# Top-k attention and mixture of depths: the mask moved from the scores into PSUM

## The chip, the cores and the metric

The kernel runs on one core of one Trainium2 chip. The metric is the time of one execution on the device in microseconds (us). Each of the core's engines runs its own queue of instructions in order: TensorE (PE in the profile; its weight loads are PEld), VectorE (DVE), ScalarE (ACT), GpSimd (POOL), and SyncE (SP), which here only issues transfers. They wait for each other through semaphores. TensorE writes PSUM; VectorE and ScalarE read PSUM and SBUF; GpSimd works in SBUF.

## What is computed

Eight batches, eight heads, 576 tokens, head width 64. In each row of the attention scores only the 32 largest entries survive, the rest is set to a very low value, and a softmax and the product with v follow. The heads are put side by side to rows of 512, and a "mixture of depths" layer picks 128 tokens in each batch by a gate score and adds a two-layer perceptron to them.

```python
scores = scale * np.matmul(q, k.transpose(0, 1, 3, 2))
kth = np.partition(scores, -top_k, axis=-1)[..., -top_k:-top_k + 1]
scores = np.where(scores >= kth, scores, -1000000000.0)
attn = np.exp(scores - max); attn /= sum(attn)
x = matmul(attn, v), heads side by side                # (8, 576, 512)
top_idx = 128 tokens with the largest x @ w_gate       # in each batch
out = x;  out[top_idx] += sigmoid(gate) * (relu(x[top_idx] @ w1) @ w2)
```

Everything is float32.

## The kernel before, in words

**Tiles.** The 576 query tokens of a batch are cut into four tiles of 128 (`t` = 0 to 3) and one of 64 (`t` = 4). A *unit* is one tile for one pair of heads: 8 batches x 5 tiles x 4 pairs = 160 units, 20 to a batch. A unit of a 128-token tile holds two score tiles of 128 x 576, one for each head; a unit of the 64-token tile packs both heads into the partitions of one score tile. So there are 288 score tiles in all.

**Steps.** The main loop (line 664) runs over steps `n`. In each step several units are worked on, each at another stage. A unit `u` passes through:

- step u-1: `multiply` (line 258): TensorE makes the scores in PSUM (`ps`); `keep` (line 275): ScalarE copies them to SBUF (`sc`);
- step u: `find_bound` (line 285): VectorE finds a bound below which few candidates lie, by many MAX8 and MATCH_REPLACE8 instructions on strips; `cut` (line 306): ScalarE rounds it into `seen`;
- step u+1: `part` (line 313): ScalarE takes the Sign of each score against the bound (`sides`) and the count; GpSimd multiplies scores by it (`y`) and appends 8 filler columns (`fill`, line 328); `find_kth` (line 337): one MAX8 of VectorE on each tile gives eight values, the last of them the 32nd largest score; `lift` (line 344): GpSimd multiplies it by 2^90 (BIG) into `seen`;
- step u+2 (lines 724 to 737): ScalarE makes Relu(2^90 (kth - score)), GpSimd subtracts it from the scores: `z`, the masked scores;
- step u+3: `turn` (line 347) and `turn_last` (line 355): TensorE transposes z into PSUM (`ptr`; the last columns into a corner of `ps`); ScalarE applies exp on the way out (`pT`, `last`);
- step u+4: `values` (line 365): TensorE multiplies by v (`av`); `keep_values` (line 401): ScalarE copies that to `xs`.

The scores are scaled down by 2^-20 when q is loaded, and exp's scale undoes it; they are not shifted by their row maximum. With v stands a column of ones, which gives the softmax's sum.

**Order.** `pe`, `dve`, `act`, `pool` and `sp` are wrappers (class `InOrder`, line 34) that pin each instruction behind the one traced before it on its engine, so every engine's queue runs in the order of the code. For ScalarE a step is: Signs of n-1, exps of n-3, copies that were put off (`flush`), Relus of n-2, score copies of n+1, value copy of n-4, cut of n. For TensorE: for each of two score tiles, transposes of n-3 and values of n-4; then scores of n+1; then a piece of the mixture or of the next batch's load. For GpSimd: y of n-1, fill, z of n-2, normalising, lift. For VectorE: bound of n, 32nd largest of n-1, then the small work of gates, normalising and routing. PSUM holds one buffer each for scores, values and the small pieces and two for transposes.

**Beside the units.** The loads of the next batch's k and q (`load_kq`, line 170) are cut into nine pieces with TensorE transposes, one each in the steps of `load_at`; v follows at step `v_at` of the batch. When a batch's last tile is normalised and its gates are known, it is stored to DRAM, and `mixture` (line 492) is run in pieces, one a step: route, pick, gather with an indirect transfer, two matmul layers in four and three pieces, and an indirect add into the output.

**The end.** After the loop a chain of checks (`sure`) looks at the smallest and largest of the recorded bounds, counts and sums; where they could not be trusted, a general routine (line 852) computes everything again. It is not entered with these inputs.

Of the kernel before, what the change touches and what calls it, by code (L numbers as in the profile page):

```python
# [9 lines left out]
AF = mybir.ActivationFunctionType  # L10
ALU = mybir.AluOpType
# [7 lines left out]
CAP = 128  # L19
# [26 lines left out]
def kernel(  # L46
# [56 lines left out]

    NS = B * NHP * (2 * J + 1)
    seen = const.tile([P, 3, NS], FP32, name="seen")
# [205 lines left out]
    def part(i, sc, at, sides):  # L313

        act.activation(
            sides[:, i, :],  # L320
            sc[:, i, :],
            AF.Sign,
            bias=seen[:, 0, at + i : at + i + 1],
            scale=-(1.0 + 2.0**-23),
            accum_out=seen[:, 2, at + i : at + i + 1],
        )

    def fill(n, y, at):

        pool.tensor_tensor(  # L330
            y[:, 0:n, S : S + 8],
            steps[:, 0:n, :],
            seen[:, 2, at : at + n].unsqueeze(2).to_broadcast([P, n, 8]),
            ALU.subtract,
        )

    def find_kth(n, y):

        next8 = stats.tile([P, 2, 8], FP32, name="next8")
        for i in range(n):  # L340
            dve.max(next8[:, i, :], y[:, i, :])
        return next8

    def lift(n, next8, at):
        pool.tensor_scalar_mul(seen[:, 1, at : at + n], next8[:, 0:n, 7], BIG)

    def turn(i, z):

        tr = ps_tr.tile([P, 512], FP32, name="ptr")
        for c in range(J):  # L350
            at = c * P + i * R
            pe.transpose(tr[:, c * P : (c + 1) * P], z[:, i, at : at + P], ident)
        return tr

    def turn_last(n, z, ps):

        last = z.rearrange("p i s -> p (i s)")[:, JP : JP + n * R]  # L360
        tr = ps[0 : n * R, 1, 1, 512 - P : 512]
        pe.transpose(tr, last, ident)
        return tr
# [91 lines left out]
    def break_ties(t, gate, gate_row, rank):  # L455

        n = R if t == J else P
        work = wkpool.tile([P, 2, S], FP32, name="ties", tag="z")
        tok_row = modpool.tile([P, S], I32, name="tok_row", tag="scratch")
        nc.gpsimd.iota(  # L460
            tok_row[:, 0:JP].rearrange("p (j i) -> p j i", j=J),
            pattern=[[1, J], [J, P]],
            base=0,
            channel_multiplier=0,
        )
        nc.gpsimd.iota(
            tok_row[:, JP:S], pattern=[[1, R]], base=JP, channel_multiplier=0
        )
        nc.vector.tensor_copy(out=work[:, 0, :], in_=tok_row)
        tok = stats.tile([P, 2], FP32, name="tok")  # L470
        nc.vector.tensor_copy(out=tok[0:n, 0:1], in_=tok_i[0:n, t : t + 1])
        nc.vector.tensor_scalar(
            out=work[0:n, 1, :],
            in0=gate_row[0:n, :],
            scalar1=gate[0:n, t : t + 1],
            scalar2=None,
            op0=ALU.is_equal,
        )
        nc.vector.scalar_tensor_tensor(
            out=work[0:n, 0, :],  # L480
            in0=work[0:n, 0, :],
            scalar=tok[0:n, 0:1],
            in1=work[0:n, 1, :],
            op0=ALU.is_lt,
            op1=ALU.mult,
            accum_out=tok[0:n, 1:2],
        )
        nc.vector.tensor_tensor(
            rank[0:n, t : t + 1], rank[0:n, t : t + 1], tok[0:n, 1:2], ALU.add
        )  # L490

    def mixture(row0, x, gate, rank, exact=False):
# [9 lines left out]
        pick = modpool.tile([P, NT, CAP], FP32, name="pick")  # L502
# [140 lines left out]
    load_at = (1, 2, 3, 4, 7, 8, 9, 11, 12)  # L643
    first_load_at = (5, 6, 7, 8, 9, 10, 11, 12, 13)
    v_at = 6
    mix_from = 5
# [12 lines left out]
    scs, bests, zs, weights = {}, {}, {}, {}  # L659
# [4 lines left out]
    for n in range(-1, len(units) + 6):  # L664
# [10 lines left out]
        if tiles_of(n - 3):  # L675
            pT = ptpool.tile([P, 2, J, P], FP32, name="pT")
            last = ptpool.tile([P, P], FP32, name="last")
            z, trs = zs.pop(n - 3), []
        if tiles_of(n - 4):
            b4, t4, hp4 = units[n - 4]  # L680
            av = ps_av.tile([P, 512], FP32, name="av")
        if tiles_of(n - 3) or tiles_of(n + 1):
            ps = room_for_scores()
        for i in range(2):
            if i < tiles_of(n - 3):
                trs.append(turn(i, z))
                if i == tiles_of(n - 3) - 1:
                    trs.append(turn_last(i + 1, z, ps))
            if i < tiles_of(n - 4):
                values(t4, hp4, i, *weights[n - 4], av, qkv[b4][2])  # L690
# [6 lines left out]
        if tiles_of(n - 1):  # L697
# [8 lines left out]
            next8 = find_kth(tiles_of(n - 1), y)  # L706
        if tiles_of(n - 3):
            w = tiles_of(n - 3)
# [8 lines left out]
            weights[n - 3] = pT, last  # L717
# [4 lines left out]


        if tiles_of(n - 2):
            sc = scs.pop(n - 2)
            z = wkpool.tile([P, 2, S], FP32, name="z")
            at = first_tile[n - 2]
            for i in range(tiles_of(n - 2)):
                act.activation(
                    z[:, i, :],  # L730
                    sc[:, i, :],
                    AF.Relu,
                    bias=seen[:, 1, at + i : at + i + 1],
                    scale=-BIG,
                )
                pool.tensor_tensor(z[:, i, :], sc[:, i, :], z[:, i, :], ALU.subtract)
            zs[n - 2] = z
        if tiles_of(n + 1):
            scs[n + 1] = keep(tiles_of(n + 1), ps)
        if tiles_of(n - 4):  # L740
            b, t, hp = b4, t4, hp4
# [5 lines left out]
            weights.pop(n - 4)  # L747
# [10 lines left out]
        b, i = divmod(n, per_batch)  # L758
        if i >= mix_from or b > 0:
            next(mixing, None)  # L760
# [6 lines left out]
        if tiles_of(n - 4):  # L767
            b, t, hp = units[n - 4]
            if hp == NHP - 1:
                normalising = b, t, xs, x, gate  # L770
        if tiles_of(n - 1):
            lift(tiles_of(n - 1), next8, first_tile[n - 1])
        b, i = divmod(n, per_batch)
        if n >= 0 and b + 1 < B:
            steps_of_load = first_load_at if b == 0 else load_at
            if i == steps_of_load[0] - 1:
                qkv[b + 1] = room_for_qkv(b + 1)
                loading = load_kq(k[b + 1], q[b + 1], *qkv[b + 1][0:2])
                next(loading)
            if i in steps_of_load:  # L780
                next(loading)
            if i == v_at:
                load_v(v[b + 1], qkv[b + 1][2])
# [8 lines left out]
    for what, op, than, limit in (  # L792
        (seen[:, 0, :], ALU.min, ALU.is_gt, LEAST),
        (seen[:, 1, :], ALU.min, ALU.is_gt, LEAST * BIG),
        (seen[:, 2, :], ALU.max, ALU.is_lt, float(MIDDLE)),
        (seen[:, 2, :], ALU.min, ALU.is_gt, float(MIDDLE - 16)),
# [27 lines left out]
    def general_weights(n, sc):  # L824

        p = wkpool.tile([P, 2, S], FP32, name="p", tag="z")
        for i in range(n):
            cur, tops = sc[:, i, :], []
            left = wkpool.tile([P, 2, S], FP32, name="left", tag="z")
# [100 lines left out]
```

## Time and profile before

| | us |
|---|---|
| median of 3 runs | 1160.65 (1156.92 to 1163.18) |
| the profiled execution's own time | 1161.06 |
| its span (first to last instruction) | 1158.6 |
| TensorE / VectorE busy | 985.9 (85%) / 910.0 (79%) |
| ScalarE / GpSimd busy | 879.7 (76%) / 905.8 (78%) |
| granted TensorE clock, mean | 0.878 of full |
| transfers | 42 GB/s mean |

Groups of instructions that the change touches (busy time in all, mean length of one):

| engine, instruction | count | busy us | mean ns |
|---|---|---|---|
| GpSimd, subtraction z | 288 | 407.7 | 1434 |
| GpSimd, lift (two columns / one) | 128 / 32 | 37.4 / 7.4 | 292 / 231 |
| GpSimd, product y | 288 | 363.0 | 1279 |
| ScalarE, Relu z | 288 | 210.5 | 783 |
| ScalarE, Sign | 288 | 221.1 | 768 |
| TensorE, transposes of z (`ptr`) | 1152 | 206.5 | 308 |
| TensorE, transposes of the last columns (`ps`) | 160 | 48.4 | 305 and 292 |

The reader should know four things. Nearly every line of the profile says L42, since all of it goes through the wrapper; the tiles' names tell the groups apart. A group's busy time is a union: where instructions of other groups overlap, both are counted, and on the pipelined TensorE the mean length of one is longer than the spacing of two. "idle before, releaser" tells for what an engine waited. The clock row tells how much of TensorE's full clock was granted; at 0.5 its matmuls take twice as long.

### The profile page before, as it was taken

What the parts mean: (1) busy time and instruction counts of PE and PEld (TensorE: products, weight loads), DVE (VectorE), ACT (ScalarE), POOL (GpSimd) and SP (SyncE); (2) the same over time, 40 slices, a digit from 0 to 9 for tenths busy, and PEclk for the clock granted to TensorE, in tenths of its full rate; (3) what the DMA queues carried; (4) which work ended last, traced back from release to release, by engine and by line L of the source; (5) the groups of instructions that cost most, each with busy time, mean ns of one, the idle gap of its engine ahead of it and who ended that gap; (6) DMA issues with size and microseconds to landing.
All of it is one profiled execution on the core that took longest, in us unless ns stands there. A gap on an engine that the chain in (4) does not pass through costs nothing.

```text
span 1158.6 us, 23113 instructions
## 1 busy us (share of the span) xinstructions
PE 985.9 (85%) x6906; PEld 820.3 (71%) x6906; DVE 910.0 (79%) x4980; ACT 879.7 (76%) x2113; POOL 905.8 (78%) x974
## 2 busy tenths in 40 slices
PE   6788878899789988899888998889987898778946
PEld 3566657787677876778677786678766787667845
DVE  5888788787897778976898868978789777898640
ACT  4898798696978769777786878969797876978721
POOL 3999798797978769777787878879797887878820
PEclk9898897799977989779886899969998788978978
DMA  5641022100411013110141101410041001000020
GB/s 121 199 100 28 1 80 63 36 2 11 114 38 29 1 17 108 38 28 1 21 114 28 28 1 34 119 28 11 9 110 26 10 1 47 5 1 10 1 60 13
DMA packets 123829, 49.03 MB, mean 42 GB/s; under 512 B 118960, under 2 KB 118960, under 8 KB 122672
## 3 DMA queue, kind: packets, MB, share of 16 engines
q1 hardware_dynamic: 120320, 42.88, 14.4%
q0 software_dynamic: 1792, 4.20, 2.1%
q8 instruction: 58, 0.95, 0.3%
q14 instruction: 75, 0.61, 0.2%
q10 hardware_dynamic: 1584, 0.39, 0.2%
HBM read 35.91 MB, written 11.53 MB: 41 GB/s over the span
## 4 chain that ended last, share of the span: by engine, by line
PE 51%; ACT 20%; POOL 19%; DVE 5%; issue 4%; DMA 1%; POOLq 0%; ACTq 0%
PE av L42 18%; PE ps L42 13%; POOL y L42 9%; PE ptr L42 9%; POOL z L42 8%; PE h_ps L42 6%; ACT sides L42 6%; ACT sc L42 5%; PE y_ps L42 4%; ACT pT L42 3%; ACT z L42 3%; PE extra_ps L42 2%; DVE prod L42 1%; DVE next L42 1%; POOL out_dram L607 1%
## 5 line engine op out<-in xcount | busy, mean ns | idle before, releaser
L42 POOL TENSOR_TENSOR z<-sc,z 128x576 f32<-128x576 f32 x288 | 407.7, 1434 | 62.9 <-ACT z L42 61.9
L42 POOL TENSOR_TENSOR y<-sc,sides 128x576 f32<-128x576 f32 x288 | 363.0, 1279 | 116.9 <-ACT sides L42 109.1
L42 DVE MAX8 cand<-sc 128x8 f32<-128x72 f32 x2304 | 323.5, 216 | 89.9 <-ACT sc L42 89.4
L42 PE MATMUL av<-v,pT 128*128 128x65 f32 (+1 forms) x2560 | 340.9, 283 | 5.5 <-ACT xs L42 5.2
L42 PEld LDWEIGHTS av<-v,pT 128*128 128x128 f32 (+1 forms) x2560 | 324.2, 203 | 18.4 <-ACT xs L42 10.2
L42 PE MATMUL ptr<-ident,z 128*128 128x128 f32 x1152 | 206.5, 308 | 113.7 <-POOL z L42 113.7
L42 DVE MAX8 next<-y 128x8 f32<-128x584 f32 x288 | 207.8, 759 | 98.9 <-POOL y L42 97.6
L42 PE MATMUL ps<-kT,qT 64*128 64x288 f32 (+1 forms) x1280 | 232.4, 488 | 21.3 <-ACT last L42 16.6
L42 ACT COPY sc<-ps 128x576 f32<-128x576 f32 x288 | 171.7, 647 | 99.6 <-PE ps L42 99.5
L42 PEld LDWEIGHTS ptr<-ident,z 128*128 128x128 f32 x1152 | 146.0, 159 | 142.4 <-POOL z L42 139.1
L42 ACT ACTIVATE pT<-ptr 128x512 f32<-128x512 f32 x288 | 163.0, 585 | 88.4 <-PE ptr L42 87.8
L42 ACT ACTIVATE sides<-sc,seen 128x576 bf16<-128x576 f32 x288 | 221.1, 768 | 4.9
L42 ACT ACTIVATE z<-sc,seen 128x576 f32<-128x576 f32 x288 | 210.5, 783 | 1.4 <-POOL seen L42 1.4
L42 PEld LDWEIGHTS ps<-kT,qT 64*128 64x128 f32 (+1 forms) x1280 | 119.5, 203 | 73.2 <-ACT last L42 30.2
L42 DVE MAX8 best<-cand 128x8 f32<-128x64 f32 x864 | 154.2, 215 | 3.3
L42 DVE MATCH_REPLACE8 cand<-best,cand 128x64 f32<-128x64 f32 x576 | 116.5, 209 | 0.0
L42 PEld LDWEIGHTS h_ps<-xeT,w 128*128 128x128 f32 x512 | 64.7, 205 | 16.6 <-issue 11.8
L42 DVE CUSTOM_DVE_ANT_0 prod<-x,wg 128x512 f32<-128x512 f32 (+1 forms) x40 | 72.1, 1802 | 4.5 <-POOL x L42 4.5
L42 PE MATMUL h_ps<-xeT,w 128*128 128x128 f32 x512 | 70.9, 296 | 2.1 <-ACT hT L42 1.4
L42 PE MATMUL y_ps<-w,hT 128*128 128x192 f32 (+1 forms) x384 | 62.2, 315 | 1.5 <-ACT gy L42 1.1
L42 PE MATMUL av<-vpair,last 128*128 128x130 f32 x256 | 63.4, 333 | 0.0
L42 PEld LDWEIGHTS y_ps<-w,hT 128*128 128x128 f32 x384 | 56.1, 190 | 10.1 <-issue 7.7
(74 smaller groups left out, 859.3 us busy)
## 6 DMA issues: line engine op xcount, KB each, us to landing
rows<-in_k_dram SPq DMA_DIRECT2D x64, 128.0 KB, 2.8
v<-in_v_dram SPq DMA_DIRECT2D x64, 128.0 KB, 3.0
out_dram<-x SPq DMA_DIRECT2D x8, 1024.0 KB, 4.7
rows<-in_q_dram SPq DMA_DIRECT2D x62, 128.0 KB, 2.9
w<-in_moe_w_dram SPq DMA_DIRECT2D x2, 2048.0 KB, 14.0
last<-in_k_dram SPq DMA_DIRECT2D x8, 128.0 KB, 3.1
vlast<-in_v_dram SPq DMA_DIRECT2D x8, 128.0 KB, 3.7
vpair<-in_v_dram SPq DMA_DIRECT2D x16, 64.0 KB, 3.1
```

The source lines that it names most:

```text
L42: return lambda *a, **kw: self._tc.keep_in_program_order(fn(*a, **kw))
L607: nc.gpsimd.indirect_dma_start(out=out.flatten_outer_dims(), out_offset=bass.IndirectOffsetOnAxis(ap=row_i, axis=0), in_=gy, in_offset=Non ...
```

## The change

The scores are no longer masked in SBUF. A new `mask` makes a small bf16 tile `less` in the step of the turn: for a unit's first score tile ScalarE takes Relu(kth - score), which is positive where the score lies below the 32nd largest and zero elsewhere; for the second score tile GpSimd compares (`is_lt`, 1 or 0). TensorE transposes the unmasked scores, and behind each transpose one bf16 matmul of `less` with a constant `out_of_reach` (the identity times -2^90) adds the transposed mask to the same place in PSUM; exp then gives zero for what is masked. The 32nd largest values are read straight from `next8`, now one constant tile for all units; `lift` is gone, and `seen` holds two rows.

A unit's stages become five: scores, bound, part, mask and turn, values. The stage of z falls away, so the turn is done at u+2 and the values at u+3. The order on ScalarE in a step is: the mask's Relu of n-2, Signs of n-1, exps of n-2, copies that were put off, score copies of n+1, value copy of n-3, cut of n. On GpSimd: comparison of n-2, y of n-1, fill, normalising. On TensorE each transpose is followed by its mask matmul. Loads and mixture come one step earlier relative to the batch, the mixture's start is no longer held back by `mix_from`, and the bookkeeping of the load steps is written as a table. Some tiles' buffers are shared otherwise (`pick` with `hT`, the general routine's tiles with `y`).

```diff
+    out_of_reach = const.tile([P, P], BF16, name="out_of_reach")
+    nc.vector.tensor_scalar_mul(out_of_reach, ident, -BIG)
...
-    seen = const.tile([P, 3, NS], FP32, name="seen")
+    seen = const.tile([P, 2, NS], FP32, name="seen")
+    next8 = const.tile([P, NS, 8], FP32, name="next8")
...
-    def find_kth(n, y):
-
-        next8 = stats.tile([P, 2, 8], FP32, name="next8")
+    def find_kth(n, y, at):
+
         for i in range(n):
-            dve.max(next8[:, i, :], y[:, i, :])
-        return next8
-
-    def lift(n, next8, at):
-        pool.tensor_scalar_mul(seen[:, 1, at : at + n], next8[:, 0:n, 7], BIG)
-
-    def turn(i, z):
+            dve.max(next8[:, at + i, :], y[:, i, :])
+
+    def mask(n, sc, at):
+
+        less = wkpool.tile([P, 2, S], BF16, name="less")
+        for i in range(n):
+            kth = next8[:, at + i, 7:8]
+            if i == 0:
+                act.activation(less[:, i, :], sc[:, i, :], AF.Relu, bias=kth, scale=-1.0)
+            else:
+                pool.tensor_scalar(
+                    out=less[:, i, :],
+                    in0=sc[:, i, :],
+                    scalar1=kth,
+                    scalar2=None,
+                    op0=ALU.is_lt,
+                )
+        return less
+
+    def turn_some(tr, z, less):
+
+        pe.transpose(tr, z, ident)
+        if less is not None:
+            pe.matmul(
+                tr, less, out_of_reach, start=False, stop=True, skip_group_check=True
+            )
+
+    def turn(i, z, less=None):
...
         for c in range(J):
-            at = c * P + i * R
-            pe.transpose(tr[:, c * P : (c + 1) * P], z[:, i, at : at + P], ident)
+            at = slice(c * P + i * R, (c + 1) * P + i * R)
+            turn_some(
+                tr[:, c * P : (c + 1) * P],
+                z[:, i, at],
+                None if less is None else less[:, i, at],
+            )
...
-    load_at = (1, 2, 3, 4, 7, 8, 9, 11, 12)
+    load_at = (0, 1, 2, 3, 6, 7, 8, 10, 11)
...
-    for n in range(-1, len(units) + 6):
+    for n in range(-1, len(units) + 5):
...
-        if tiles_of(n - 3):
+        if tiles_of(n - 2):
+            sc, trs = scs.pop(n - 2), []
+            less = mask(tiles_of(n - 2), sc, first_tile[n - 2])
             pT = ptpool.tile([P, 2, J, P], FP32, name="pT")
             last = ptpool.tile([P, P], FP32, name="last")
-            z, trs = zs.pop(n - 3), []
...
         for i in range(2):
+            if i < tiles_of(n - 2):
+                trs.append(turn(i, sc, less))
+                if i == tiles_of(n - 2) - 1:
+                    trs.append(turn_last(i + 1, sc, ps, less))
             if i < tiles_of(n - 3):
-                trs.append(turn(i, z))
-                if i == tiles_of(n - 3) - 1:
-                    trs.append(turn_last(i + 1, z, ps))
-            if i < tiles_of(n - 4):
-                values(t4, hp4, i, *weights[n - 4], av, qkv[b4][2])
+                values(t3, hp3, i, *weights[n - 3], av, qkv[b3][2])
...
-
-        if tiles_of(n - 2):
-            sc = scs.pop(n - 2)
-            z = wkpool.tile([P, 2, S], FP32, name="z")
-            at = first_tile[n - 2]
-            for i in range(tiles_of(n - 2)):
-                act.activation(
-                    z[:, i, :],
-                    sc[:, i, :],
-                    AF.Relu,
-                    bias=seen[:, 1, at + i : at + i + 1],
-                    scale=-BIG,
-                )
-                pool.tensor_tensor(z[:, i, :], sc[:, i, :], z[:, i, :], ALU.subtract)
-            zs[n - 2] = z
...
-        b, i = divmod(n, per_batch)
-        if i >= mix_from or b > 0:
-            next(mixing, None)
+        next(mixing, None)
...
-        if tiles_of(n - 1):
-            lift(tiles_of(n - 1), next8, first_tile[n - 1])
```

## The prediction

> **What bounds the kernel now.** I read the page first (engines, then the chain that ended last), then the waits, then the timelines of ScalarE and TensorE through single steps, and last the busy time and granted clock in stretches of 3.41 us. Engines and chain:
>
> ```profile
> PE 985.9 (85%) x6906; PEld 820.3 (71%) x6906; DVE 910.0 (79%) x4980; ACT 879.7 (76%) x2113; POOL 905.8 (78%) x974
> ...
> PE 51%; ACT 20%; POOL 19%; DVE 5%; issue 4%; DMA 1%; POOLq 0%; ACTq 0%
> ```
>
> Four engines are nearly equally busy and the chain runs through three: no single engine is the bound, so a loop between them must be looked for. The waits (total, times, longest):
>
> ```profile
> PE ptr L42 <- POOL z L42: 113.7, 85, 3.9
> ...
> ACT sc L42 <- PE ps L42: 99.5, 71, 3.3
> ```
>
> TensorE's largest wait is for the masked scores z that GpSimd finishes; ScalarE's largest of this kind is for fresh scores in PSUM. One step of ScalarE (start, duration) in the stretch where the next batch is loaded:
>
> ```profile
> 439.05 0.78 ACT L42 ACTIVATE sides<-sc,seen 128x576 bf16<-128x576 f32 x1
> ...
> 441.53 0.27 ACT L42 ACTIVATE last<-ps 128x128 f32<-128x128 f32 x1
> 441.69 0.60 ACT L42 ACTIVATE qT<-tr 128x512 f32<-128x512 f32 x1
> 442.17 1.45 ACT L42 ACTIVATE z<-sc,seen 128x576 f32<-128x576 f32 x2
> 443.50 1.19 ACT L42 COPY sc<-ps 128x576 f32<-128x576 f32 x2
> 444.55 0.31 ACT L42 COPY xs<-av 128x130 f32<-128x130 f32 x1
> 444.70 0.24 ACT L42 CAST seen<-best 128x2 f32<-128x2 bf16 x1
> 444.98 0.78 ACT L42 ACTIVATE sides<-sc,seen 128x576 bf16<-128x576 f32 x1
> ```
>
> ScalarE has no gap: the step is 444.98 - 439.05 = 5.93 us, and ScalarE's own work fills it. GpSimd is as full there (2.52 for y, 0.22 for the fill, 2.78 for z, 0.21 for the lift: 5.73). TensorE waits 0.8 to 1.7 us in such a step. In the steps that carry a first expert matmul TensorE has no gap and the step is 527.05 - 521.00 = 6.05 us:
>
> ```profile
> 521.00 0.60 PE L42 MATMUL ptr<-ident,z 128*128 128x128 f32 x4
> 521.44 1.00 PE L42 MATMUL av<-v,pT 128*128 128x65 f32 x8
> 522.28 0.61 PE L42 MATMUL ptr<-ident,z 128*128 128x128 f32 x4
> 522.72 0.27 PE L42 MATMUL ps<-ident,z 128*128 128x128 f32 x1
> 522.83 1.00 PE L42 MATMUL av<-v,pT 128*128 128x65 f32 x8
> 523.67 0.44 PE L42 MATMUL av<-vpair,last 128*128 128x130 f32 x2
> 524.04 1.19 PE L42 MATMUL ps<-kT,qT 64*64 64x288 f32 x8
> 525.16 2.05 PE L42 MATMUL h_ps<-xeT,w 128*128 128x128 f32 x16
> ```
>
> From start to start: four transposes 0.44 (0.11 each), one tile's values 0.84, the last columns 0.11, second values with the pair matmul 1.21, scores 1.12, experts 1.9. These are full-clock figures. Stretches of 3.41 us (PE busy first, granted clock third from the end):
>
> ```profile
> 315.34:318.75 3.41, 1.76 (x18) 1.39 (x15) 3.41 (x21) 3.38 (x9) 3.41 (x4) 1.00 0.39 89
> 318.75:322.17 3.41, 3.41 (x18) 3.36 (x17) 3.41 (x29) 2.85 (x8) 3.25 (x6) 0.50 0.01 2
> ```
>
> A stretch in which TensorE was busy 1.76 us is followed by one at half clock. Over the whole trace, cut where the clock changes: of 35 full-clock stretches with PE busy up to 1.80 us, 28 were followed by half clock; of 12 with 1.8 to 2.3, one; above that, none. A fall mostly lasts two stretches (6.8 us). At half clock a step takes 8 to 10 us, so a middle batch of 20 steps takes 139.8 us (batches 3 and 4, between the first Signs of their steps) where full-clock rows would give some 123.
>
> **The change, part by part.**
>
> *ScalarE.* Per step with two tiles it loses one Relu of two: 0.7 us (1.45 for two in a row), 128 times, some 90 us of busy time. The other Relu stays at 0.78 (the same elements; bf16 out as in the Sign row), but moves from between exp and the copies to the head of the next step: behind the copies of new scores, the copy of values and the cut, ahead of the Signs.
>
> *GpSimd.* It loses two subtractions and the lift, 2.78 + 0.21, and gets one comparison of 576 columns. No row shows it: at least the 0.2 of the 16-column fill, at most the 1.43 of a two-input z; I take 0.8, the middle. Even at 1.43 GpSimd sums to 2.52 + 0.22 + 1.43 + 0.26 (its share of normalising) = 4.4 us a step. It costs nothing: its eighth-best value is there when VectorE ends the step before, over 2 us ahead of the second tile's turn. If that cover were gone it would delay the second tile by at most 1.43.
>
> *TensorE* gains nine bf16 matmuls with weight loads in a two-tile step, five in a one-tile step: 1312 in all. None is in the trace. Upper end: the 0.11 of an fp32 transpose of the same shape. Lower end: the eight 64x64 fp32 transposes (0.66 for x8, 0.23 the last one's own length: 0.06 apart), which load as many bytes of weights per row as 128 bf16 columns. Both are equally near; I take 0.08, that is 0.72 a step.
>
> *The units* lose a stage: masks and turn fall together. So a new wait arises. TensorE's first mask matmul waits for ScalarE's Relu of the same step; behind it in order stand the second tile's transposes, the values and the scores of the next unit. The Relu stands on ScalarE behind the copy of scores that TensorE's last matmuls of the previous step made. A closed loop, once a step:
>
> - first mask matmul to end of scores: 521.00 to 524.04 + 1.19 is 4.23, less the first transpose (0.11, done while waiting), plus 0.72: 4.84;
> - TensorE to ScalarE 0.04 (scores end 556.14, copy starts 556.18);
> - copies to the Relu: 443.50 to the cut's start 444.70 is 1.20, plus 0.16 (as `last` at 441.53 lets the next in at 441.69); the Relu does not wait for the cut's result as the Sign did: 1.36;
> - Relu 0.78, and 0.04 to TensorE.
>
> Sum 7.05 us, where ScalarE alone needed 5.93 and needs about 5.2 after. ScalarE's other route (Signs 1.72, exps 1.23, then scores may be written) ends 0.3 us before TensorE arrives there, so it does not bind. VectorE's 5.7 a step (910.0 over 160) is covered too; without this cover it would only matter below 5.7.
>
> By step of a batch: twelve steps at 7.05 = 84.6; the two-head tiles at the batch's end shorten the loop (turn by 0.76, values 0.32, copy 0.53): 5.97 three times and 6.73 once; where TensorE's own work is longer it sets the step: first expert layer 0.88 + 0.64 + 0.19 + 2.05 + 1.12 + 1.95 = 6.83 twice, second layer 7.60 and 6.84. Together 137.3 us, 6.865 a step.
>
> *Loads and mixture* move one step earlier with the values; the load issues on SP and the indirect transfers on GpSimd keep their places behind the same work, rows of k and q land 2.8 us after their issue and are used a step or more later, and GpSimd has gained time for its 1.6 us indirect issues: nothing. The new constant costs one VectorE instruction before the loop, where loads are awaited: nothing. The tail loses one step: 1104.28 to 1108.70 between the last two turns, 4 us.
>
> *The clock.* In the loop TensorE idles 2.22 us in one piece, less what stands behind the scores: the four load, route or gather transposes and the first transpose of the next step (0.70 by modelled ends) leave 1.52, so a 3.41 us stretch keeps at least 1.89 busy: by the counts above it falls about once in twelve. Steps with nothing behind the scores leave about 2.1 us (23: eight in the first batch, nine in the last, one in each other) and fall about six times in ten, when one stretch holds the gap. With some two from the load steps that is 16 falls; each halves about 6 us of TensorE's work, 3 us on the loop: 48 us.
>
> Sum against the profiled execution (span 1158.6, its own time 1161.06, median of the runs 1160.65): 22.0 to the first Sign, 159 x 6.865 = 1091.5, tail 61.2 - 4 = 57, falls 48: 1218.5, plus 2.5 around the span, about 1221.
>
> [...]
>
> **The rivals.**
>
> *A, the clock stays up:* gaps of 1.5 us lie under the 1.8 us edge, and even the long ones may be split between stretches. Against it: the full-clock stretches that fell. Time 1173; with the mask matmul at 0.06 the loop loses 0.18 in some 143 steps: 1147; at 0.11: 1212.
>
> *B, the load steps fall too:* if activity is counted without the modelled ends of matmuls, 1.52 is nearer 1.7. Then some 46 falls more, 3 us each: about 1360.
>
> *C, the other side: the loop does not close.* What speaks for it: masks are ready over 2 us before they are wanted, GpSimd and ScalarE are relieved of 2.2 and 0.7 us, and TensorE's largest wait disappears. If the Relu were issued ahead of the copies, steps would be VectorE's 5.7 and TensorE's own 6.8 to 7.6 with experts: 13 x 5.7 + 47.5 = 121.6 a batch, about 1050. It decides once the loop is under 6.45 us a step (1155 less 2.5, 22, 57 and 48, over 159). Against it: ScalarE's row runs in the order of the code.
>
> **How the numbers follow.** Forecast (1175 to 1290) 0.56; A 0.22, B 0.14, C 0.08. A runs from 1147 to 1175: four tenths of it are faster by over 0.5% (below 1155), a quarter the same. Faster 0.08 + 0.09 = 0.17, same 0.06, slower 0.77; 0.5% is about what a measurement of this kernel can tell from no change. The range leaves out C and most of B: 1135 to 1300.
>
> **What would show it.** Right: TensorE's first mask matmul waits on ScalarE's `less` for over 1.5 us in nearly every step without experts, ScalarE waits on `ps` each step, the wait on z is gone, GpSimd falls below 60%, Sign-to-Sign is near 7.05 at full clock. Wrong: Sign-to-Sign below 6.5 in load steps, or a mask pair far from 0.08, or a mean clock far from 0.878 either way.

## The result, and the profile after

The changed kernel takes 1329.07 us (median of 4 runs, 1321.82 to 1335.56), the kernel before 1158.79 us in the same series (4 runs, 1156.0 to 1163.18): a ratio of 1.146, 95% interval 1.139 to 1.154. It is slower, as forecast, but by 170 us and not 60, and lies above the forecast's range of 1135 to 1300. The profiled execution took 1335.56 us, its span is 1333.6, its mean granted clock 0.855. In the experiments, runs over 1.5% above the fastest of their kernel are in the medians given but not in the ratios.

Engines and chain of the changed kernel:

```profile
PE 1116.1 (84%) x8218; PEld 909.1 (68%) x8218; DVE 862.7 (65%) x4981; ACT 790.5 (59%) x1985; POOL 687.9 (52%) x654
...
PE 74%; ACT 21%; issue 2%; DVE 1%; POOL 1%; DMA 1%; SPq 0%; ACTq 0%; POOLq 0%
```

ScalarE and GpSimd lost the work that the diff takes from them, and every engine's share of the longer span fell, TensorE's least (85% to 84%). GpSimd has all but left the chain (19% to 1%), which now alternates between TensorE and ScalarE. The waits of the changed kernel (total, times, longest):

```profile
ACT sc L42 <- PE ps L42: 328.6, 153, 4.9
PEld L42 <- ACT less L42: 207.2, 127, 3.8
...
PE ptr L42 <- ACT less L42: 175.8, 121, 3.5
```

TensorE (PE and its weight loads, PEld) waits for ScalarE's mask, and ScalarE for TensorE's scores, each about once a step: the two halves of one loop. One turn of it in a load step, first ScalarE of the changed kernel (start, duration, idle before):

```profile
514.60 0.60 ACT L42 ACTIVATE qT<-tr 128x512 f32<-128x512 f32 x1
516.53 1.18 ACT L42 COPY sc<-ps 128x576 f32<-128x576 f32 x2 [1.32 <-PE ps L42]
517.60 0.29 ACT L42 COPY xs<-av 128x130 f32<-128x130 f32 x1
517.75 0.22 ACT L42 CAST seen<-best 128x2 f32<-128x2 bf16 x1
517.85 0.80 ACT L42 ACTIVATE less<-sc,next 128x576 bf16<-128x576 f32 x1
```

and TensorE of the changed kernel in the same stretch:

```profile
511.59 0.23 PE L42 MATMUL ptr<-out_of_reach,less 128*128 128x128 bf16 x1 [1.50 <-ACT less L42]
...
515.19 1.24 PE L42 MATMUL ps<-kT,qT 64*128 64x288 f32 x8
516.36 0.66 PE L42 MATMUL tr<-ident,rows 128*128 128x128 f32 x4
516.85 0.27 PE L42 MATMUL ptr<-ident,sc 128*128 128x128 f32 x1
518.70 0.23 PE L42 MATMUL ptr<-out_of_reach,less 128*128 128x128 bf16 x1 [1.57 <-ACT less L42]
518.77 0.28 PE L42 MATMUL ptr<-ident,sc 128*128 128x128 f32 x1
518.88 0.22 PE L42 MATMUL ptr<-out_of_reach,less 128*128 128x128 bf16 x1
518.94 0.28 PE L42 MATMUL ptr<-ident,sc 128*128 128x128 f32 x1
```

Scores end at 516.43, the copy starts 0.10 later, the Relu at 517.85, and the first mask matmul at 518.70. TensorE's previous mask matmul was at 511.59: the turn is 518.70 - 511.59 = 7.11 us, against 7.05 forecast. At full clock nearly every load or plain step has just this length. What the forecast missed is how seldom the clock is full. The changed kernel in stretches of 3.41 us (PE busy first, granted clock third from the end):

```profile
589.18:592.59 3.41, 3.41 (x28) 2.59 (x26) 1.43 (x4) 1.77 (x4) 1.86 (x2) 1.00 0.00 0
592.59:596.01 3.42, 1.84 (x20) 1.73 (x20) 3.28 (x27) 3.42 (x10) 1.81 (x2) 1.00 0.36 81
596.01:599.42 3.41, 3.41 (x20) 2.99 (x18) 2.15 (x8) 1.41 (x4) 1.75 (x3) 0.50 0.00 0
599.42:602.83 3.41, 3.41 (x14) 2.10 (x13) 0.76 (x5) 1.02 (x2) 1.98 (x1) 0.50 0.00 0
602.83:606.25 3.42, 2.41 (x25) 2.19 (x25) 3.42 (x29) 3.09 (x9) 1.13 (x1) 1.00 0.01 2
```

The stretch with TensorE busy 1.84 us, one load step's gap in one piece, is followed by two at half clock. Such a stretch recurs all through: 25 full-clock stretches lie between 1.8 and 1.9 us, and 19 of them were followed by half clock; between 1.9 and 2.3, 3 of 36. In the main loop the clock falls to half 39 times and stays there for 365 us (before: 29 and 263).

**The sum again, by its own terms** (span forecast 1218.5, measured 1333.6, difference 115):

| term | forecast | measured |
|---|---|---|
| to the first Sign | 22.0 | 22.6 |
| 159 steps at full clock | 1091.5 | some 1100 |
| sigmoid's wait in the mixture (not in the forecast) | 0 | 12 |
| half clock | 48 | some 144 |
| tail | 57 | 54.7 |

How the second row and the fourth come about: for each place in a batch the shortest of its eight steps is taken as the step at full clock; these sum to 1097.1 over 159 steps. Some 16 us are added for two places whose shortest step stands in the first or last batch and lacks work that the others have: mainly the nineteenth, 4.75 us in the last batch and 7.00 in six others. The ninth step is 8.68 us or more in every batch, because some of it always runs at half clock; 1.57 x 8 = 12.6 us of it is counted with the clock. The rest of the loop's 1256.3 us, some 143, is excess over these steps: seven times 1.72 us of the sigmoid's wait, shown below, and the clock, since nearly all of it beside that wait lies in steps that ran in part at half clock.

### The profile page after: what moved, and what is told of

It reads as the page before. It is cut to its first block, busy times and chain, and to the rows that moved or that the text cites. A ratio compares the mean times of both kernels' runs of the same rounds, so it can differ in the third digit from the quotient of the medians.

```text
span 1333.6 us, 25265 instructions
## 1 busy us (share of the span) xinstructions
PE 1116.1 (84%) x8218; PEld 909.1 (68%) x8218; DVE 862.7 (65%) x4981; ACT 790.5 (59%) x1985; POOL 687.9 (52%) x654
## 4 chain that ended last, share of the span: by engine, by line
PE 74%; ACT 21%; issue 2%; DVE 1%; POOL 1%; DMA 1%; SPq 0%; ACTq 0%; POOLq 0%
PE av L42 28%; PE ps L42 20%; PE ptr L42 18%; ACT sc L42 11%; ACT less L42 6%; PE y_ps L42 4%; PE h_ps L42 3%; ACT xs L42 2%; ACT seen L42 1%; PE extra_ps L42 1%; DVE pick L42 0%; PE tr L42 0%; DMA rows<-in_k_dram 0%; ACT pT L42 0%; DVE junk L42 0%
## 5 line engine op out<-in xcount | busy, mean ns | idle before, releaser
L42 PE MATMUL ptr<-out_of_reach,less 128*128 128x128 bf16 x1152 | 243.2, 239 | 177.3 <-ACT less L42 175.8
L42 PE MATMUL av<-v,pT 128*128 128x65 f32 (+1 forms) x2560 | 365.7, 294 | 0.4 <-ACT xs L42 0.4
L42 PEld LDWEIGHTS av<-v,pT 128*128 128x128 f32 (+1 forms) x2560 | 335.9, 209 | 10.6 <-issue 1.4
L42 POOL TENSOR_SCALAR less<-sc,next 128x576 bf16<-128x576 f32 x128 | 228.5, 1785 | 150.2 <-DVE next L42 138.2
L42 PEld LDWEIGHTS <-less 128*128 128x128 bf16 (+1 forms) x1312 | 143.7, 112 | 213.7 <-ACT less L42 207.2
L42 PE MATMUL ptr<-ident,sc 128*128 128x128 f32 x1152 | 277.6, 309 | 0.0
L42 PE MATMUL ps<-kT,qT 64*128 64x288 f32 (+1 forms) x1280 | 242.6, 506 | 7.4 <-ACT last L42 5.3
L42 PEld LDWEIGHTS ptr<-ident,sc 128*128 128x128 f32 x1152 | 188.6, 164 | 31.1 <-issue 13.6
L42 ACT ACTIVATE less<-sc,next 128x576 bf16<-128x576 f32 x160 | 126.2, 789 | 0.0
L42 POOL TENSOR_TENSOR x<-xs,rden 128x512 f32<-128x512 f32 (+1 forms) x40 | 41.6, 1041 | 85.5 <-DVE rden L42 83.6
```

What stands on the lines that cost most here:

```text
L42: return lambda *a, **kw: self._tc.keep_in_program_order(fn(*a, **kw))
```

## The experiments

Theories before the first runs. L: the loop of scores, copies, Relu and mask is the loss, in two ways, its own length and the 1.6 us of TensorE idle in one piece that halve the clock. M: the 1312 bf16 matmuls cost far more than their spacing says. G: GpSimd's comparison, 1785 ns where 0.2 to 1.43 was the bound, holds up y and with it VectorE.

### The masks made a stage earlier

Masks and turn are taken apart again: ScalarE makes `less` between the scores and their copy, one step ahead of the turn; units have six stages and the loads the old places.

```diff
-        if tiles_of(n - 2):
-            less = mask(tiles_of(n - 2), sc, first_tile[n - 2])
+        if tiles_of(n - 3):
+            less = lesses.pop(n - 3)
...
+        if tiles_of(n - 2):
+            lesses[n - 2] = mask(tiles_of(n - 2), scs[n - 2], first_tile[n - 2])
         if tiles_of(n + 1):
             scs[n + 1] = keep(tiles_of(n + 1), ps)
```

> Theory L (the closed loop): the changed kernel is slow because ScalarE's mask stands behind the copies of scores that TensorE's last matmuls feed, and TensorE's next turn waits for that mask; the clock falls in the gap this leaves. Here the mask matmuls, both masks and all engines' work stay, but the masks are made one step before the turn (units of six stages). L: the wait on less goes, Sign-to-Sign in a load step drops from 7.11 to about 5.8 (VectorE's 5.7), few clock falls, time about 1065. Rival M (the 1312 added bf16 matmuls cost what was lost): their number is unchanged, so the time stays above 1280. Rival G (GpSimd's 1.79 us comparison delays y and so VectorE): stays above 1250, since GpSimd's work is the same.

Measured: 1101.36 us (1096.5 to 1106.22), ratio to the kernel before 0.950 (0.941 to 0.959). All matmuls and comparisons of the change are still there, so M and G fall; one stage of distance turns 15% slower into 5% faster. Engines of this kernel:

```profile
PE 997.0 (91%) x8218; PEld 830.1 (76%) x8218; DVE 854.6 (78%) x4981; ACT 798.3 (73%) x1985; POOL 678.5 (62%) x654
```

and its ScalarE in a load step:

```profile
434.76 1.18 ACT L42 COPY sc<-ps 128x576 f32<-128x576 f32 x2 [0.81 <-PE ps L42]
...
438.87 0.60 ACT L42 ACTIVATE qT<-tr 128x512 f32<-128x512 f32 x1
439.35 0.79 ACT L42 ACTIVATE less<-sc,next 128x576 bf16<-128x576 f32 x1
440.57 1.18 ACT L42 COPY sc<-ps 128x576 f32<-128x576 f32 x2 [0.43 <-PE ps L42]
```

The Relu now stands in the time in which ScalarE waits for scores, and TensorE's largest stop in the step is 0.24 us, for the single buffer of values. The load step is 440.57 - 434.76 = 5.81 us (expected 5.8), the falls are 10 and the half clock 96 us. The 36 us above the expected total are more than covered by two routing steps of the mixture, 10.6 and 9.0 to 11.6 us in seven batches (62 us above 5.8 each), where most falls of the clock stayed.

### Five stages kept, masks issued ahead of the score copies

```diff
+        if tiles_of(n - 1):
+            lesses[n - 1] = mask(tiles_of(n - 1), scs[n - 1], first_tile[n - 1])
         if tiles_of(n + 1):
             scs[n + 1] = keep(tiles_of(n + 1), ps)
```

> The changed kernel, five stages kept, but the masks for the next step's turn are issued ahead of the copies of scores on ScalarE, so the turn does not wait for a Relu behind them. L: the loop through the copies opens; the next one runs through VectorE (copy, bound 3.8, 32nd largest 0.76, Relu 0.83, copy: about 6.4 us), so about 1125 with a few clock falls. M and G: unchanged, above 1280.

Measured: 1192.0 us (1190.18 to 1207.49), ratio 1.032 (1.020 to 1.044); step 6.73 us, 16 falls, 123 us at half clock. The old loop is broken, and another takes its place; the waits of this kernel:

```profile
ACT less L42 <- DVE next L42: 208.6, 136, 2.9
POOL less L42 <- DVE next L42: 161.3, 92, 2.4
```

In five stages the eighth-best value is found in the very step in which the moved Relu wants it, so ScalarE stands still for VectorE and the score copies behind it. This is the loop that the expectation named; it was put at 6.4 and measures 6.73. What makes the earlier version fast is the stage, not only the order.

### TensorE kept busy: more transposes in the gap

The transposes of loads, routing and gather, which stand in the gap behind the scores, are done three times to the same place; steps with none get twelve of the identity. Nothing on the loop is touched.

```diff
+    REP = 3
...
-            for c in range(J):
+            for c in REP * tuple(range(J)):
                 pe.transpose(
...
+        if not late and tiles_of(n - 2):
+            idle = ps_misc.tile([P, 512], FP32, name="idle", tag="misc")
+            for c in REP * tuple(range(J)):
+                pe.transpose(idle[:, c * P : (c + 1) * P], ident, ident)
```

> The changed kernel with more TensorE work in the gap: each transpose group of loads, routing and gather is done three times to the same place, and steps that leave nothing behind the scores get twelve transposes of the identity. That is 0.9 to 1.3 us more TensorE work in about 13 steps of each batch. Theory L with the clock: the loop is not lengthened (the gap is 1.5 to 2.2 us), the windows no longer fall below 1.9 us busy, and the half-clock time of 365 us shrinks to that caused by the sigmoid step: time about 1215, faster by some 110 although work was added. If half clock is not what the gap costs, the time is unchanged or longer: 1330 to 1430.

Measured: 1266.64 us (1258.29 to 1278.26), ratio 1.096 (1.084 to 1.108): 62 us faster for added work. The loop is as long as it was, 7.11 us, but the gap is not; TensorE of this kernel in a load step:

```profile
503.69 1.24 PE L42 MATMUL ps<-kT,qT 64*128 64x288 f32 x8
504.87 1.53 PE L42 MATMUL tr<-ident,rows 128*128 128x128 f32 x12
506.23 0.27 PE L42 MATMUL ptr<-ident,sc 128*128 128x128 f32 x1
507.21 0.23 PE L42 MATMUL ptr<-out_of_reach,less 128*128 128x128 bf16 x1 [0.70 <-ACT less L42]
```

An idle stretch of 0.70 us where 1.57 was; 15 falls (39) and 119 us at half clock (365). So the clock's term is a cause of its own and a large one. It is not all: the falls left stand in the routing steps of the mixture (seven of them in the ninth step), and the step of the sigmoid has grown to 10.6 to 11.0 us.

The same filler in the kernel before:

> The kernel before with the same filler. If half clock costs the kernel before some 16 us a batch, as its 139.8 us batches against 123 us of full-clock steps say, the filler brings the time from 1159 to about 1070. If its steps are bound by ScalarE and GpSimd alone and the clock is only a symptom, the time stays within 1%: 1150 to 1170, or gets longer by what the filler pushes.

Measured: 1149.04 us (1145.19 to 1152.51), ratio 0.991 (0.987 to 0.994); 19 falls (29), 164 us at half clock (263). A hundred us less at half clock bought 12 us, or 17 within the loop, since the filler also moves the first Sign from 22.0 to 28.3 us. The likely reason, which no run tests apart, is that there ScalarE and GpSimd fill their step, so that a slow TensorE is largely hidden, while in the changed kernel TensorE is on the loop in every step.

### The sigmoid's exponentials put off

ScalarE of the changed kernel in the eighth step of a batch:

```profile
255.05 0.22 ACT L42 CAST seen<-best 128x2 f32<-128x2 bf16 x1
255.16 0.21 ACT L42 ACTIVATE sig<-sig 128x4 f32<-128x4 f32 x1
256.77 0.20 ACT L42 ACTIVATE sig<-sig 64x1 f32<-64x1 f32 x1 [1.40 <-DVE sig L42]
256.88 0.76 ACT L42 ACTIVATE less<-sc,next 128x576 bf16<-128x576 f32 x1
```

Two small exponentials of the mixture stand between the cut and the Relu, and the second waits 1.40 us for VectorE, which has the `pick` masks between its two clamps. The step is 8.83 us in place of 7.11. Here they are computed at the mixture's start and put off to the next step's `flush`.

```diff
+            late.append(
+                lambda o=sig[0:n, t0:t1]: act.activation(o, o, AF.Exp, scale=-1.0)
+            )
         yield from route(gate, rank, exact)
...
-            act.activation(sig[0:n, t0:t1], sig[0:n, t0:t1], AF.Exp, scale=-1.0)
```

> The changed kernel with one piece of the mixture moved: the sigmoid's exps no longer stand on ScalarE between the cut and the mask's Relu (where they wait for VectorE in the middle), but are put off into the next step's copies, four steps earlier in the batch. Theory L: that step (8.83 us in seven batches) falls back to 7.11, and the clock falls that follow it (six of 39 begin in the step after) go: 12 us plus 20 to 30, so about 1290. If the wait for the sigmoid is hidden, 1329.

Measured: 1307.35 us (1290.27 to 1310.69), ratio 1.118 (1.108 to 1.128), with the eighth step down to 7.11 in three of the four batches where its clock is full (8.21 in the other); 35 falls, 328 us at half clock. A second, smaller cause: with the falls that followed it 22 us by the medians, 33 by the ratios (1.146 to 1.118).

Both together, filler and late exponentials:

> Filler and late sigmoid together in the changed kernel: the loop stays, both causes of gaps over 1.5 us are filled or removed. L: hardly any half clock, steps at their floors (about 133 a batch): 22 + 1062 + 55 + 2, about 1150 to 1175. If half clock has another cause than the gaps, above 1230 (the filler alone gave 1267).

Measured: 1239.04 us (1230.05 to 1240.1), ratio 1.062 (1.054 to 1.069), 14 falls, 99 us at half clock. By its total this is the rival's side (above 1230), but the half clock did go, from 365 to 99 us. That is the loop nearly by itself: the shortest step of each place sums to 133.7 us a batch, and 89 us of excess over these are left. Of them 46 lie in the sixth, eighth and tenth steps of a batch, which hold pieces of the routing with little filler or none, and 33 in the second, eighteenth and nineteenth, whose shortest step stands in the first or last batch and lacks work that the others have. The expected 1150 to 1175 took all of these at their shortest.

### Each mask matmul twice, and one in four

To price the mask matmuls, each is issued twice:

```diff
-            pe.matmul(
-                tr, less, out_of_reach, start=False, stop=True, skip_group_check=True
-            )
+            for _ in range(2):
+                pe.matmul(
+                    tr, less, out_of_reach, start=False, stop=True, skip_group_check=True
+                )
```

> The changed kernel with every mask matmul issued twice (the masked scores get twice -2^90; the result is the same). L: on the loop at the price of a transpose and mask pair, 0.17 less 0.11, that is 0.06 us each at full clock and 0.12 at half: 0.5 to 0.7 us a step, 1329 becomes about 1420. M: if the first 1312 cost the 170 us lost, the second cost as much again, 1500. If the mask matmuls hide behind the transposes' weight loads, 1335.

Measured: 1313.9 us (1308.05 to 1337.81), ratio 1.126 (1.117 to 1.134). The step grew as L says, from 7.11 to 7.61, nine times 0.056 us:

```profile
505.03 0.29 PE L42 MATMUL ptr<-out_of_reach,less 128*128 128x128 bf16 x2 [1.50 <-ACT less L42]
505.15 0.28 PE L42 MATMUL ptr<-ident,sc 128*128 128x128 f32 x1
505.27 0.28 PE L42 MATMUL ptr<-out_of_reach,less 128*128 128x128 bf16 x2
```

(TensorE of this kernel: a pair and a transpose every 0.23 us, where one and a transpose took 0.17.) But the total did not grow by the 70 us or so that this makes (0.50 in each of 128 steps, about half of it in the other 32); of the expected totals 1335, that of hidden matmuls, is the nearest, though they are not hidden. There are 29 falls, 27 of them of a single stretch, and 106 us at half clock where the changed kernel has 365; of its 39 falls 23 lasted two stretches and ten longer. In the kernel with the doubled masks 10 of 32 stretches with 1.8 to 1.9 us busy fell.

The other side leaves work out: the mask is added behind only the first of a tile's four transposes, and 384 columns of each tile stay unmasked.

```diff
-                None if less is None else less[:, i, at],
+                None if less is None or c else less[:, i, at],
```

> The changed kernel with the mask matmul behind only the first of a tile's four transposes (the other 384 columns of each tile stay unmasked, so that much of the computation is left out): six bf16 matmuls fewer in a two-tile step, the wait of TensorE for the first mask as it was. At 0.056 each the step goes from 7.11 to 6.77, and the steps at full clock from 137.9 to about 132 a batch. If the clock's share stays as in the changed kernel (365 us at half clock, 159 us above the full-clock steps) the time is about 1285. If what the doubled masks showed holds the other way too (TensorE's activity between two waits decides how often the clock falls and how soon it is back), the loop's gain is given back by more or longer falls: over 400 us at half clock and 1310 to 1360. If the mask matmuls cost nothing between the transposes, the step stays 7.11 and the time 1330.

Measured: 1295.07 us (1279.66 to 1300.27), ratio 1.107 (1.097 to 1.117). The step is 6.69, shorter by 0.42 or 0.07 for each of six matmuls. So the price of one mask matmul is 0.06 to 0.07 from both sides, about 0.6 us a step. The profiled execution, 1299.77 us, has 31 falls of up to nine stretches and 399 us at half clock (365 in the changed kernel). That less work in the loop means more half clock is not shown by it: of the four runs this and one more have a mean granted clock of 0.838 and 0.834, but the other two, 1279.66 and 1290.36 us, have 0.858 and 0.864, where the changed kernel's four have 0.855 to 0.871. They lie to both sides of the 1285 expected for an unchanged share of half clock.

### Both masks by ScalarE

```diff
-            if i == 0:
+            if i < 2:
                 act.activation(less[:, i, :], sc[:, i, :], AF.Relu, bias=kth, scale=-1.0)
```

> The changed kernel with both masks made by ScalarE: GpSimd's comparison (1785 ns, above the 0.2 to 1.43 that was forecast) is gone, ScalarE gets a second Relu of 0.78 behind the first. If GpSimd's comparison is hidden and the loop runs through the first Relu alone, the step stays 7.11 (the second Relu ends near 504.6 where TensorE wants it at 506.56; the second exp has 1.40 us of waiting to give), the first mask wait stays, and the time is that of the changed kernel, 1315 to 1345. If the long comparison holds up the loop through y and VectorE, steps shorten by some 0.3 or more and the time falls below 1290. If ScalarE's own row binds (Signs and exps 0.7 later), the step is 7.4 or more and the time over 1360.

Measured: 1295.39 us (1286.27 to 1303.2), ratio 1.116 (1.110 to 1.122). The step is 7.05, as the first theory has it to within 0.06, and the third (ScalarE's own row) is refuted: it waits for scores as before. But the total, expected at 1315 to 1345, is 34 us lower than the changed kernel's. At full clock the steps explain some 5 us of that (0.05 in twelve steps, 0.67 less in the seventeenth, 0.66 more in the batch's first). The rest comes with the clock: 29 falls and 246 us at half clock, with 12 of 26 stretches of 1.8 to 1.9 us falling where 19 of 25 did. So GpSimd's long comparison costs the loop almost nothing, and a shift of 0.06 us in a loop that sits on the clock's edge goes with some 30 us. That these stretches fall less often goes in part with the place of the gap in them: see the last section.

### A version that beats both kernels

The six stages with the late exponentials and the copy of values ahead of the score copies, so that TensorE's single buffer of values comes free sooner:

```diff
+        if tiles_of(n - 4):
...
+            keep_values(t, hp, av, xs)
         if tiles_of(n + 1):
             scs[n + 1] = keep(tiles_of(n + 1), ps)
```

> Units of six stages (the masks made a step before the turn), the sigmoid late, and the copy of values ahead of the copies of scores, since in the six-stage run TensorE waited for that copy in the single buffer of values (28 us, 87 times). L: steps of 5.81 go to VectorE's 5.6, the routing steps of 10.6 and 9 to 12 us to about 7: about 1050. If the copy of values does not bind, 1065; if the routing steps are bound by VectorE's own work, 1085.

Measured: 1070.56 us (1064.04 to 1072.92), ratio 0.918 (0.912 to 0.924). The engines of this kernel:

```profile
PE 986.2 (92%) x8218; PEld 830.7 (78%) x8218; DVE 864.2 (81%) x4981; ACT 800.4 (75%) x1985; POOL 680.8 (64%) x654
```

and two lines of its ScalarE, one step apart:

```profile
645.75 0.59 ACT L42 COPY kT<-tr 128x512 f32<-128x512 f32 x1
...
651.21 0.60 ACT L42 ACTIVATE qT<-tr 128x512 f32<-128x512 f32 x1
```

A load step is 5.46 us, 1.65 less than the five-stage loop. The tenth step, at 9.9 us, and what follows it hold most of what is left over (7 falls, 89 us at half clock). So the mask in PSUM, shared by ScalarE and GpSimd, is compatible with a gain of 8%, with one stage more and these two reorderings. The mask's own share is better read from the first experiment, 5%, which has as many stages as the kernel before and the exponentials in their old place: the kernel before waits for the same exponentials (shown below), and putting them off there was not run.

## Why the prediction was right and wrong

**Direction and mechanism: right.** "A closed loop, once a step" is what the chain shows, and the version with the mask a stage earlier shows it by removing it. The loop was forecast at 7.05 and measured 7.11: TensorE's part 4.84 as worked out (511.59 to 516.43), the hand-over 0.10 (forecast 0.04), the copies to the Relu 1.32 (1.36), the Relu to TensorE 0.85 (0.82). That the 4.84 fits exactly is luck: the nine masks took some 0.5 where 0.72 was put, while each tile's values took 0.90 and the scores 1.24 where the rows before have 0.84 and 1.19. The steps with expert layers are 6.5 to 6.7 and 7.0 to 7.1 (6.83; 7.60 and 6.84), and those with two-head tiles at the end of a batch 5.98 (5.97). The waits named beforehand all appeared, and the wait for z is gone.

**ScalarE: right.** 879.7 to 790.5 us busy, 89 less (90 forecast).

**GpSimd: wrong in size, right that it is covered.** The comparison takes 1785 ns, above the upper end of 1.43: a two-input f32 subtraction was no bound for a one-input comparison that writes bf16. It costs nothing all the same within 0.06 us a step: with the comparison gone from GpSimd the loop stayed.

**Mask matmuls: right.** Forecast 0.08 within 0.06 to 0.11; the spacing of transpose and mask is 0.17, so 0.06, and the doubled and thinned masks give 0.056 and 0.07. The changed kernel's loads of `less` last 112 ns in the mean, but beside other work: a mask matmul with its load adds only these 0.056 to 0.07 us to the loop.

**The failed step is "16 falls; each halves about 6 us of TensorE's work, 3 us on the loop: 48 us".** There were 39 falls, worth some 144 us, 3.7 us each. Two things were wrong in it. First, the chance of a fall for a load step was taken as "about once in twelve" from the stretches of 1.8 to 2.3 us in the kernel before. That band held twelve stretches, only two of them at the lower end, where the forecast itself had put the load steps (1.89 busy). The edge lies inside the band: 19 of 25 below 1.9, 3 of 36 above. Second, a fall was taken to last two stretches; ten of the 39 lasted three to eight. Nine of these ten hold a stretch with a gap at half clock too, but two go on through five and six stretches in a row in which TensorE was busy throughout, so what ends a fall stays open. Rival B said just this ("the load steps fall too", 1360), and with a chance of 0.14 it was put too low: a sum that sets 12 steps of each of eight batches at 0.09 us from an edge read off two stretches had to carry both cases as nearly equal. The measured time is nearer to B than to the forecast; the number of falls, 39, is halfway between the forecast's 16 and B's 62.

**A missed step: loads and mixture at "nothing".** The mixture moved one step earlier and was looked at for its queues, but not for the two exponentials on ScalarE, which in the changed kernel stand ahead of the Relu that TensorE waits for: 1.72 us in each of seven batches, 12 us, and 22 to 33 with the falls behind them. The wait itself is not new. ScalarE of the kernel before in the ninth step of a batch:

```profile
205.48 0.20 ACT L42 ACTIVATE sig<-sig 128x4 f32<-128x4 f32 x1 [2.87 <-DVE sig L42]
207.00 0.20 ACT L42 ACTIVATE sig<-sig 64x1 f32<-64x1 f32 x1 [1.32 <-DVE sig L42]
207.11 0.76 ACT L42 ACTIVATE sides<-sc,seen 128x576 bf16<-128x576 f32 x1
```

In the kernel before these waits add up to 36 us over the eight batches. The exponentials hold up the Signs there, and this step takes 10.41 us in most batches where plain ones take 5.93. So the 139.8 us of a middle batch, which the prediction sets against some 123 as the cost of half clock, hold 4.5 us of this wait, and the sum of the steps left it out.

## What to carry to other kernels

Taking out a stage saves nothing if it sets the maker of a value and its reader into the same turn of two in-order queues: the loop that closes is as long as everything between (here 7.11 us a step), and a stage of distance cost nothing here and was worth 17% (1329 to 1101 us). A gap that recurs in every step must be weighed against the clock's edge (here TensorE busy about 1.9 us of 3.41: 19 of 25 stretches just below it fell, 3 of 36 above) with the counts closest to its own length, and where these are few, both outcomes belong in the range; where the gap lies in the clock's stretches counts as well as its length (here 50 of 55 fell where it began early, none of 39 where it began late). Then look for every small instruction that stands ahead of the one on the loop, above all in steps that are moved.

## What the runs showed of the hardware

**The clock's edge.** In five-stage loops with a gap of 1.5 to 1.6 us, full-clock stretches with TensorE busy 1.8 to 1.9 us of 3.41 fell in 19 of 25 cases (changed kernel), 20 of 33 (late exponentials), 12 of 26 (both masks by ScalarE), 10 of 32 (masks doubled); with 2.3 us and more, hardly ever (2 of 193 in the changed kernel). Which of them fall goes with where the gap lies in the stretch. In these four traces and that of the thinned masks, 50 of 55 such stretches fell where the gap began within 0.35 us of the stretch's start, 13 of 31 where it began up to 0.9 us behind it, and none of 39 where it began later (in seven the gap began before the stretch). The early place is that of 18 of the 25 in the changed kernel, 14 of the 26 with both masks by ScalarE, 9 of the 32 with doubled masks. Each load step moves the gap on by what it is longer than two stretches: 0.28 us at 7.11, 0.22 at 7.05, 0.78 at 7.61. Why an early gap counts for more was not tested; the matmuls that share the stretch with it differ too. No stretch had to be idle throughout: the one from 592.59 us in the changed kernel fell with a gap of 1.58 us and 1.84 us busy. Added fp32 transposes alone took the falls from 39 to 15 and the half clock from 365 to 119 us.

**More work, less half clock.** 1312 more bf16 matmuls in the loop took the half clock from 365 to 106 us (mean granted clock 0.934 to 0.958 in its four runs, 0.855 to 0.871 in the changed kernel's); leaving out 864 did not move it clearly. The longer step shifts the gap in the stretch, which can account for fewer falls; why 27 of the 29 lasted only one stretch stays open.

**VectorE beside GpSimd.** The gate's product of two SBUF tensors on VectorE, with no change to it:

```profile
253.82 0.67 DVE L42 CUSTOM_DVE_ANT_0 prod<-x,wg 128x512 f32<-128x512 f32 x1
```

In the changed kernel all forty take 0.67 us, though GpSimd's comparison runs beside 31 of them for 0.39 us; in the six-stage kernel it runs beside eight from start to end, and they take 0.67 us as well. In the kernel before, 37 of the forty ran beside GpSimd's two-input subtraction z, and those took 1.2 to 2.4 us, mostly 1.9; the other three took 0.67 to 0.69. So the product was slowed beside the subtraction and took the same 0.67 us beside the one-input comparison; why was not tested.

**A one-input comparison on GpSimd**, 128 x 576 f32 to bf16 against a value per partition, took 1.72 us in the median and 1.79 in the mean in the changed kernel, longer than the subtraction of two f32 tensors in the kernel before (1.43 in the mean).
